# Fewer products of zeros ahead of the first FFN block: 33 in place of 60

## The chip, the cores and the metric

The kernel runs on one core of a Trainium2 chip. Its time is the device time of one execution in microseconds (us); lower is better. The median of three runs of the kernel before is 180.96 us (180.59 to 181.47).

## What is computed

Windowed attention with a few global keys, and then a feed-forward network (FFN) that takes the largest of three products:

```python
# q, k, v: 4 batches x 8 heads x 768 x 64; n_global = 8, n_local = 96
keep = is_global | is_local                  # key < 8, or 0 <= query - key < 96
scores = q @ k.T / 8 - slope[head] * dist    # dist: distance, 96 for a global key out of the window
a = softmax(where(keep, scores, -1e9))
x = (a @ v) with the heads side by side      # 3072 x 512
h = maximum(maximum(x @ w1, x @ w2), x @ w3) # 3072 x 768
out = h @ w_out                              # 3072 x 512, float32
```

## The kernel before, in words

The 3072 rows are 24 tiles of 128 queries, six to a batch. A tile needs its own 128 keys and those of the tile before it; the global keys are copied over rows of the tile before that no query of the tile can see. FFN work goes by chunks of 4, 2, 2, 4, 4, 4 and 4 tiles, so that one weight block meets up to 512 rows at once.

No planner runs at build time. The whole order of the work is one string, `SCHEDULE` (lines 24 to 86), and the last loop (lines 518 to 524) issues its units one after the other. Each unit is a letter for a function, its arguments, and behind an @ the slot of the ring of buffers that it takes. Every engine works off its own instructions in this order; between engines, semaphores hold an instruction until its inputs are there and its buffer is free. The loads are all issued from SP's queue, also in this order.

The units that the steps below speak of:

- `l` loads q, k or v (lines 182 to 195), `w` a weight (455 to 460). `c` and `v` cast them to bf16 (197 to 213); `W` casts a slice of a weight (462 to 464), W1.2 the middle block of the third weight.
- `x` transposes q or k on TensorE (PE) through an identity (219 to 233), and `y` copies the result out of PSUM (235 to 244). For the first two pairs of tiles, four rows at a time lie side by side and the tile is called tpq.
- `S` makes scores of four heads (a group g) of one tile T: S1.0 is group 0 of tile 1 (279 to 296). Where its last argument is 1 ("biased"), two products with the identity first put the distance bias into PSUM. `e` takes the exponential on ScalarE (ACT) (298 to 303). `m` multiplies by a mask on VectorE (DVE), and only where the group was not biased (305 to 313).
- `V` copies the global rows of v into a tile's v, on ACT or GpSimd (POOL) (268 to 275). `A` multiplies the weights of a tile by its v and the v of the tile before (326 to 341), `n` divides by the sums on DVE (343 to 350), `t` transposes the result on PE and `u` copies it to xT (359 to 367).
- `F` is one FFN product of a chunk: four matmuls into one PSUM bank (374 to 380). `f` takes it out of PSUM, as a copy or as a maximum (387 to 399). `O`, `o` and `s` are the product with w_out, its copy and its store.
- `D` and `d` are products of zeros: n matmuls of a constant tile of zeros into a PSUM bank that nobody reads, of the ring h or, for `d`, of the ring sp:

```python
def u_D(slot, n, w, name="h"):
    wp = ring(name, slot, [128, 512 if name == "h" else 1024], FP32, "wp")
    for _ in range(n):
        nc.tensor.matmul(wp[:, 0:w], zeros[:, 0:128], zeros[:, 0:w], start=True, stop=True)
```

D5.256@3 so is five matmuls of 256 columns into slot 3 of h. The ring h has four PSUM banks, which transposes, FFN products and zeros share; the ring sp has two double banks, which scores and attention outputs share. A product into a bank that another instruction last wrote or read waits for that instruction.

Of the kernel before, what the change touches and what calls it, by code (L numbers as in the profile page):

```python
# [22 lines left out]

SCHEDULE = """
    l1.12.0@0 l0.12.0@1 R K3 K7 K4 B1.0 K2 K6 K1 K0 K5 B5.1 B3.1 B0.0 c1.12.0.1@0 B2.1 l1.12.1@2 l0.12.1@3
    c0.12.0.1@1 B7.1 l2.0.2@0 v1.0.2 v0.1.2 l2.1.2@1 v0.0.2 l1.2.2@4 D10.512@0 D2.256@1 x12.1.0@1 y0.1.0.0@0
    v1.1.2 y1.1.0.1@1 D5.256@2 x12.0.0@2 l0.2.2@5 y0.0.0.0 S0.0.1@0 c1.12.1.1 e0.0@0 d7.256@1 S1.0.0@1
    w0.0@0 c0.12.1.1 v3.1.2 w0.1@1 x12.1.1@3 D7.256@0 x12.0.1@0 v2.1.2 e1.0@1 y0.1.1.0 w0.2@2 y0.0.1.0
    d6.256@0 S0.1.0@0 G0.0 e0.1@2 v3.0.2 S1.1.0@1 v2.0.2 c1.2.2.2@2 e1.1@3 w1.0@0 y1.1.1.1 y1.0.0.1 y1.0.1.1
    w1.1@1 l2.2.2@2 G1.1 D4.256@1 S2.0.1@0 e2.0@4 m0.1.1 D6.256@1 A0@1 m1.0.1 n0@0 D4.256@1 S2.1.0@0 m1.1.1  # L30
    G2.0 e2.1@5 D2.256@1 S3.1.0@1 t0@1 m2.1.1 e3.1@6 u0.1@0 D5.256@3 A1@0 n1@1 S3.0.1@1 c0.2.2.1 l0.3.2@6
    V1.0 D7.256@3 A2@0 V2.2 x2.1.2@3 e3.0@7 w1.2@2 m3.1.1 x2.0.2@2 y2.1.2.0@2 A3@1 n2@2 W0.1.2 V3.2 t2@0
    n3@3 u2.1 y2.0.2.0 W0.0.2 t1@1 D5.256@3 t3@3 W2.0.2 G3.0 u1.0 l1.3.2@0 u3.1 B4.0 S4.0.0@0 S4.1.0@1
    e4.1@0 G4.0 W1.1.2 v4.1.2 q2@1 m4.1.1 e4.0@2 W0.2.0 F0.0.1@2 F0.1.1@0 F0.1.0@1 F0.0.0@3 f0.1.0.1@0
    l2.3.2@0 m4.0.1 f0.0.0.0@1 S5.1.0@1 v4.0.2 S5.0.0@0 F0.0.2@1 f0.1.1.1 F0.1.2@3 F0.4.0@0 e5.0@1 f0.0.1.1
    f0.0.2.1@0 f0.1.2.1 W1.0.0 e5.1@3 m5.0.1 W2.1.1 l1.4.2@1 F0.5.0@2 f0.5.0.1@2 c0.3.2.2@0 v5.0.0 v5.1.0
    F0.3.0@1 F0.2.0@3 f0.2.0.1@3 f0.3.0.0@4 F0.2.1@2 f0.2.1.1 A4@0 n4@0 W1.2.2 F0.5.1@3 m5.1.1 f0.5.1.1
    f0.4.0.0@1 F0.4.1@1 v7.0.2 t4@0 F0.3.1@2 x3.0.2@3 V4.0 f0.3.1.1 W2.2.0 A5@1 y3.0.2.0@3 u4.1@1 n5@2
# [519 lines left out]
```

## Time and profile before

| | us |
|---|---|
| median of three runs | 180.96 (180.59 to 181.47) |
| the profiled execution, in all | 180.58 |
| its span, from the first to the last instruction | 178.8 |
| TensorE busy | 170.8 (96%) |
| VectorE busy | 131.4 (73%) |
| ScalarE busy | 107.7 (60%) |
| GpSimd busy | 43.1 (24%) |
| zero products (L478): 10 of 512 columns, 60 of 256 | 12.1 busy, first start 1.2, last 23.4 |
| FFN products (L379), 504 | 99.6 busy, first start 24.75 |

Times are counted from the first instruction of the span. Matmuls are pipelined and their ends are modelled, so the distance from start to start tells what one costs. "Idle before" is the time in which an engine had nothing running, with what ended it. The chain of work is followed back from the last instruction, at each step to what released it; in it, "issue" is time in which an engine waited for nothing that the profile shows. PEclk is the clock that TensorE was granted, as a share of the full one.

### The profile page before, as it was taken

The numbers are of one execution on the slowest core, as the hardware profiler recorded it, in microseconds if no ns is written. First come the engines' busy times: TensorE is split into PE (matmuls) and PEld (weight loads), VectorE is DVE, ScalarE is ACT, GpSimd is POOL, SyncE is SP. The second block draws the span as 40 slices with busy tenths as digits, with TensorE's granted clock in tenths as the row PEclk, the third lists the DMA queues.
The fourth block names the chain that finished last, engine by engine and source line by source line (L and its number), as shares of the span: only waits on it lengthen the run. The fifth ranks groups of instructions, "written<-read, shape, count | busy, mean of one in ns | idle before, by whom it ended". The sixth has DMA issues, their size and how long they took to land.

```text
span 178.8 us, 3957 instructions
## 1 busy us (share of the span) xinstructions
PE 170.8 (96%) x1552; PEld 96.8 (54%) x1552; DVE 131.4 (73%) x258; ACT 107.7 (60%) x166; POOL 43.1 (24%) x72
## 2 busy tenths in 40 slices
PE   7699999999999999999999999999999999999692
PEld 2376764466876776844545544644445464444242
DVE  6558958988697979775899668997768984355800
ACT  5968898675899958866589587336154733110022
POOL 3049285427034453000202701130101040000000
PEclk9999999999999999999999999999999999999999
DMA  4999999999984999499999789997990142460006
GB/s 148 351 291 316 366 370 322 344 297 339 293 214 97 197 242 176 96 349 290 194 299 225 144 153 278 248 207 236 229 175 11 33 146 59 176 235 4 0 22 215
DMA packets 66627, 37.49 MB, mean 210 GB/s; under 512 B 24624, under 2 KB 61360, under 8 KB 66608
## 3 DMA queue, kind: packets, MB, share of 16 engines
q1 hardware_dynamic: 66464, 37.17, 83.5%
q8 instruction: 12, 0.20, 0.5%
q10 hardware_dynamic: 144, 0.07, 0.1%
q14 instruction: 7, 0.06, 0.1%
HBM read 25.17 MB, written 6.29 MB: 176 GB/s over the span
## 4 chain that ended last, share of the span: by engine, by line
PE 89%; ACT 3%; issue 2%; DVE 2%; POOL 1%; ACTq 0%
PE h L379 53%; PE po L403 18%; PE sp L295 7%; PE op L337 3%; PE wp L478 3%; PE op L340 3%; ACT wmask L324 2%; PE tp L233 1%; PE xtp L364 1%; PE tpq L227 1%; POOL qb L208 1%; ACT qkT L241 1%; ACT bias L319 0%; POOL va L273 0%; DVE ht L398 0%
## 5 line engine op out<-in xcount | busy, mean ns | idle before, releaser
L379 PE MATMUL h<-xT,w 128*128 128x512 bf16 (+1 forms) x504 | 99.6, 349 | 0.1
L379 PEld LDWEIGHTS <-w 128*128 128x128 bf16 x504 | 47.3, 98 | 42.0 <-issue 1.0
L302 ACT ACTIVATE P<-sp 128x1024 bf16<-128x1024 f32 (+1 forms) x48 | 43.9, 952 | 14.2 <-PE sp L295 13.8
L403 PE MATMUL po<-wo,ht 128*128 128x512 bf16 (+2 forms) x156 | 33.9, 363 | 1.5 <-DVE ht L398 1.5
L311 DVE TENSOR_TENSOR P<-P,wmask 128x1024 bf16<-128x1024 bf16 x38 | 28.7, 766 | 7.3 <-ACT P L302 7.2
L395 DVE TENSOR_TENSOR h<-h,h 128x512 bf16<-128x512 bf16 (+1 forms) x42 | 25.1, 606 | 10.1 <-PE h L379 7.6
L398 DVE TENSOR_TENSOR ht<-h,h 128x512 bf16<-128x512 bf16 (+1 forms) x42 | 26.4, 646 | 4.2 <-PE h L379 3.2
L393 ACT CAST h<-h 128x512 bf16<-128x512 f32 (+1 forms) x24 | 12.6, 538 | 20.9 <-PE h L379 20.7
L403 PEld LDWEIGHTS <-ht 128*128 128x128 bf16 x156 | 13.9, 98 | 15.8 <-DVE ht L398 2.0
L213 POOL CAST va<-rawv 64x512 bf16<-64x512 f32 x20 | 13.2, 664 | 28.6 <-DMA rawv<-in_v_dram 27.9
L349 DVE TENSOR_TENSOR xb<-op,rz 128x512 bf16<-128x512 f32 x24 | 16.6, 692 | 0.8
L393 DVE CAST h<-h 128x512 bf16<-128x512 f32 (+1 forms) x18 | 10.7, 597 | 8.3 <-PE h L379 8.0
L273 POOL COPY va<-vaf 4x260 int32<-4x260 int32 x20 | 8.8, 439 | 30.9 <-PE op L340 27.0
L295 PE MATMUL sp<-qkT 64*128 64x128 bf16 x352 | 14.7, 218 | 0.7 <-ACT qkT L241 0.6
L295 PEld LDWEIGHTS <-qkT 64*128 64x128 bf16 x352 | 10.0, 94 | 9.0 <-issue 6.3
L418 ACT COPY ost<-po 128x512 f32<-128x512 f32 x15 | 8.8, 587 | 8.5 <-PE po L403 8.3
L337 PEld LDWEIGHTS <-P 128*128 128x128 bf16 x192 | 12.5, 97 | 2.1 <-issue 0.2
L478 PE MATMUL wp<-zeros 128*128 128x256 bf16 (+1 forms) x70 | 12.1, 312 | 1.2 <-DVE cap L496 1.2
L337 PE MATMUL op<-va,P 128*128 128x65 bf16 x160 | 12.5, 193 | 0.0
L340 PEld LDWEIGHTS <-P 128*128 128x128 bf16 x160 | 10.5, 97 | 1.6
L340 PE MATMUL op<-va,P 128*128 128x65 bf16 x128 | 9.9, 193 | 0.1
L408 ACT COPY ost<-po 128x512 f32<-128x512 f32 (+2 forms) x5 | 2.3, 480 | 12.3 <-PE po L403 12.2
(69 smaller groups left out, 130.0 us busy)
## 6 DMA issues: line engine op xcount, KB each, us to landing
rawv<-in_v_dram SPq DMA_DIRECT2D x12, 512.0 KB, 8.0
out_dram<-ost SPq DMA_DIRECT2D x23, 256.0 KB, 2.5
rawk<-in_k_dram SPq DMA_DIRECT2D x10, 512.0 KB, 7.3
rawq<-in_q_dram SPq DMA_DIRECT2D x10, 512.0 KB, 7.4
wst<-in_moe_w_dram SPq DMA_DIRECT2D x3, 1024.0 KB, 10.3
wst<-in_moe_w_dram SPq DMA_DIRECT2D x3, 512.0 KB, 8.2
wost<-in_moe_w_out_dram SPq DMA_DIRECT2D x3, 512.0 KB, 6.6
rawqk<-in_k_dram SPq DMA_DIRECT2D x2, 512.0 KB, 5.0
```

The lines of the kernel that those rows point to most:

```text
L295: nc.tensor.matmul(sp[:, hh, j2, ds], qT(T - ds, 1)[hsl, jp], qT(T, 0)[hsl, jp], start=not how, stop=True, skip_group_check=True)
L302: nc.scalar.activation(P[:, :, 0:n], sps[T, g].rearrange("p a b d n -> p (a b) d n")[:, :, 0:n], AF.Exp, bias=0.0, scale=scale)
L311: mul(P, P, wmask[:, g, :, 0:2])
L337: nc.tensor.matmul(o, P[:, i, 0], heads(va(T))[:, h], start=True, stop=(t == 0), skip_group_check=True)
L340: nc.tensor.matmul(o, P[:, i, 1], heads(va(T - 1))[:, h], start=False, stop=True, skip_group_check=True)
L349: nc.vector.tensor_tensor(out=x.rearrange("p (g h) d -> p g h d", g=2), in0=o4[:, :, :, 0:64], in1=rz[:, :, :, None].to_broadcast([128, 2, ...
L379: nc.tensor.matmul(ps, w123[f // 2][:, j, dm, (f % 2) * 128:(f % 2) * 128 + 128], xT[c][:, dm], start=(dm == 0), stop=(dm == 3))
L393: copies[how](h01, ps)
L395: nc.vector.tensor_max(h01s[c, f], h01s[c, f], ps)
L398: nc.vector.tensor_max(dst, h01s[c, f].rearrange("p (t e i) -> p t e i", e=2, i=64), ps.rearrange("p (t e i) -> p t e i", e=2, i=64))
L403: nc.tensor.matmul(po, ht[c][:, f, tt * 128:(tt + 1) * 128], wo[:, f, cols], start=(f == 0), stop=(f == NF - 1))
L478: nc.tensor.matmul(wp[:, 0:w], zeros[:, 0:128], zeros[:, 0:w], start=True, stop=True)
```

## The change

Only counts in the schedule are changed. Eleven of the twelve units of 256-column zeros that stood ahead of the first FFN product are left, ten of them with a smaller count; d7 on slot 1 of sp, which stood between the exponential of tile 0's biased group and the scores of tile 1, is gone. The first unit, ten products of 512 columns, stays. In the order in which PE meets them:

| stands ahead of | before | after |
|---|---|---|
| first transposes of k (x12.1.0) | D2 | D1 |
| first transposes of q (x12.0.0) | D5 | D3 |
| scores S1.0, behind the biased S0.0 | d7 | none |
| transposes x12.0.1 | D7 | D5 |
| scores S0.1 | d6 | d4 |
| scores S2.0 | D4 | D3 |
| attention product A0 | D6 | D2 |
| scores S2.1 | D4 | D3 |
| scores S3.1 | D2 | D2 |
| attention product A1 | D5 | D4 |
| attention product A2 | D7 | D2 |
| transposes t3 | D5 | D4 |
| in all | 60 | 33 |

The diff, cut to the lines with a changed unit (the others only move a line break):

```diff
-    c0.12.0.1@1 B7.1 l2.0.2@0 v1.0.2 v0.1.2 l2.1.2@1 v0.0.2 l1.2.2@4 D10.512@0 D2.256@1 x12.1.0@1 y0.1.0.0@0
-    v1.1.2 y1.1.0.1@1 D5.256@2 x12.0.0@2 l0.2.2@5 y0.0.0.0 S0.0.1@0 c1.12.1.1 e0.0@0 d7.256@1 S1.0.0@1
-    w0.0@0 c0.12.1.1 v3.1.2 w0.1@1 x12.1.1@3 D7.256@0 x12.0.1@0 v2.1.2 e1.0@1 y0.1.1.0 w0.2@2 y0.0.1.0
-    d6.256@0 S0.1.0@0 G0.0 e0.1@2 v3.0.2 S1.1.0@1 v2.0.2 c1.2.2.2@2 e1.1@3 w1.0@0 y1.1.1.1 y1.0.0.1 y1.0.1.1
-    w1.1@1 l2.2.2@2 G1.1 D4.256@1 S2.0.1@0 e2.0@4 m0.1.1 D6.256@1 A0@1 m1.0.1 n0@0 D4.256@1 S2.1.0@0 m1.1.1
-    G2.0 e2.1@5 D2.256@1 S3.1.0@1 t0@1 m2.1.1 e3.1@6 u0.1@0 D5.256@3 A1@0 n1@1 S3.0.1@1 c0.2.2.1 l0.3.2@6
-    V1.0 D7.256@3 A2@0 V2.2 x2.1.2@3 e3.0@7 w1.2@2 m3.1.1 x2.0.2@2 y2.1.2.0@2 A3@1 n2@2 W0.1.2 V3.2 t2@0
-    n3@3 u2.1 y2.0.2.0 W0.0.2 t1@1 D5.256@3 t3@3 W2.0.2 G3.0 u1.0 l1.3.2@0 u3.1 B4.0 S4.0.0@0 S4.1.0@1
+    c0.12.0.1@1 B7.1 l2.0.2@0 v1.0.2 v0.1.2 l2.1.2@1 v0.0.2 l1.2.2@4 D10.512@0 D1.256@1 x12.1.0@1 y0.1.0.0@0
+    v1.1.2 y1.1.0.1@1 D3.256@2 x12.0.0@2 l0.2.2@5 y0.0.0.0 S0.0.1@0 c1.12.1.1 e0.0@0 S1.0.0@1 w0.0@0
+    c0.12.1.1 v3.1.2 w0.1@1 x12.1.1@3 D5.256@0 x12.0.1@0 v2.1.2 e1.0@1 y0.1.1.0 w0.2@2 y0.0.1.0 d4.256@0
+    S0.1.0@0 G0.0 e0.1@2 v3.0.2 S1.1.0@1 v2.0.2 c1.2.2.2@2 e1.1@3 w1.0@0 y1.1.1.1 y1.0.0.1 y1.0.1.1 w1.1@1
+    l2.2.2@2 G1.1 D3.256@1 S2.0.1@0 e2.0@4 m0.1.1 D2.256@1 A0@1 m1.0.1 n0@0 D3.256@1 S2.1.0@0 m1.1.1 G2.0
+    e2.1@5 D2.256@1 S3.1.0@1 t0@1 m2.1.1 e3.1@6 u0.1@0 D4.256@3 A1@0 n1@1 S3.0.1@1 c0.2.2.1 l0.3.2@6 V1.0
+    D2.256@3 A2@0 V2.2 x2.1.2@3 e3.0@7 w1.2@2 m3.1.1 x2.0.2@2 y2.1.2.0@2 A3@1 n2@2 W0.1.2 V3.2 t2@0 n3@3
+    u2.1 y2.0.2.0 W0.0.2 t1@1 D4.256@3 t3@3 W2.0.2 G3.0 u1.0 l1.3.2@0 u3.1 B4.0 S4.0.0@0 S4.1.0@1 e4.1@0
```

On ACT, DVE, POOL and SP the instructions and their order are the same as before.

More of the change, by code (lines that the diff above doesn't have):

```diff
@@ L25 @@
     l1.12.0@0 l0.12.0@1 R K3 K7 K4 B1.0 K2 K6 K1 K0 K5 B5.1 B3.1 B0.0 c1.12.0.1@0 B2.1 l1.12.1@2 l0.12.1@3
-    c0.12.0.1@1 B7.1 l2.0.2@0 v1.0.2 v0.1.2 l2.1.2@1 v0.0.2 l1.2.2@4 D10.512@0 D2.256@1 x12.1.0@1 y0.1.0.0@0
-    v1.1.2 y1.1.0.1@1 D5.256@2 x12.0.0@2 l0.2.2@5 y0.0.0.0 S0.0.1@0 c1.12.1.1 e0.0@0 d7.256@1 S1.0.0@1
-    w0.0@0 c0.12.1.1 v3.1.2 w0.1@1 x12.1.1@3 D7.256@0 x12.0.1@0 v2.1.2 e1.0@1 y0.1.1.0 w0.2@2 y0.0.1.0
-    d6.256@0 S0.1.0@0 G0.0 e0.1@2 v3.0.2 S1.1.0@1 v2.0.2 c1.2.2.2@2 e1.1@3 w1.0@0 y1.1.1.1 y1.0.0.1 y1.0.1.1
-    w1.1@1 l2.2.2@2 G1.1 D4.256@1 S2.0.1@0 e2.0@4 m0.1.1 D6.256@1 A0@1 m1.0.1 n0@0 D4.256@1 S2.1.0@0 m1.1.1
-    G2.0 e2.1@5 D2.256@1 S3.1.0@1 t0@1 m2.1.1 e3.1@6 u0.1@0 D5.256@3 A1@0 n1@1 S3.0.1@1 c0.2.2.1 l0.3.2@6
-    V1.0 D7.256@3 A2@0 V2.2 x2.1.2@3 e3.0@7 w1.2@2 m3.1.1 x2.0.2@2 y2.1.2.0@2 A3@1 n2@2 W0.1.2 V3.2 t2@0
-    n3@3 u2.1 y2.0.2.0 W0.0.2 t1@1 D5.256@3 t3@3 W2.0.2 G3.0 u1.0 l1.3.2@0 u3.1 B4.0 S4.0.0@0 S4.1.0@1
-    e4.1@0 G4.0 W1.1.2 v4.1.2 q2@1 m4.1.1 e4.0@2 W0.2.0 F0.0.1@2 F0.1.1@0 F0.1.0@1 F0.0.0@3 f0.1.0.1@0
-    l2.3.2@0 m4.0.1 f0.0.0.0@1 S5.1.0@1 v4.0.2 S5.0.0@0 F0.0.2@1 f0.1.1.1 F0.1.2@3 F0.4.0@0 e5.0@1 f0.0.1.1
+    c0.12.0.1@1 B7.1 l2.0.2@0 v1.0.2 v0.1.2 l2.1.2@1 v0.0.2 l1.2.2@4 D10.512@0 D1.256@1 x12.1.0@1 y0.1.0.0@0
[6 more added lines that the diff above has]
+    u2.1 y2.0.2.0 W0.0.2 t1@1 D4.256@3 t3@3 W2.0.2 G3.0 u1.0 l1.3.2@0 u3.1 B4.0 S4.0.0@0 S4.1.0@1 e4.1@0
+    G4.0 W1.1.2 v4.1.2 q2@1 m4.1.1 e4.0@2 W0.2.0 F0.0.1@2 F0.1.1@0 F0.1.0@1 F0.0.0@3 f0.1.0.1@0 l2.3.2@0
+    m4.0.1 f0.0.0.0@1 S5.1.0@1 v4.0.2 S5.0.0@0 F0.0.2@1 f0.1.1.1 F0.1.2@3 F0.4.0@0 e5.0@1 f0.0.1.1
     f0.0.2.1@0 f0.1.2.1 W1.0.0 e5.1@3 m5.0.1 W2.1.1 l1.4.2@1 F0.5.0@2 f0.5.0.1@2 c0.3.2.2@0 v5.0.0 v5.1.0
```

## The prediction

> **What bounds the kernel now.** I read the windows view first, cut at the first FFN product (24.75 us) and at the last one before the tail (168.56). Its columns are the stretch, its length, then busy time (instructions) of PE, PEld, DVE, ACT and POOL, the granted clock, DMA share and GB/s.
>
> ```profile
> 0.00:24.75 24.75, 21.69 (x269) 14.64 (x269) 18.13 (x48) 19.40 (x34) 11.36 (x24) 1.00 1.00 304
> 24.75:168.56 143.81, 143.78 (x1248) 79.11 (x1248) 111.56 (x207) 86.03 (x128) 31.73 (x49) 1.00 0.85 201
> 168.56:178.80 10.24, 5.38 (x36) 3.02 (x36) 1.71 (x3) 2.29 (x5) 0.00 (x0) 0.96 0.30 103
> ```
>
> In the middle stretch TensorE is idle 0.03 of 143.81 us: from the first FFN product on it is the bound, so whatever moves the start at 24.75 moves the end. The zero products all lie ahead of it. The chain of work that ended last (start, length, what) tells which of them count:
>
> ```profile
> 9.03 0.88 PE wp L478 x7
> 9.91 0.04 issue
> 9.96 0.40 PE sp L295 x8
> 10.36 0.55 PE tpq L227 x8
> 10.91 0.78 PE wp L478 x7
> 11.69 0.04 issue
> 11.73 0.61 PE tpq L227 x8
> 12.34 0.67 PE wp L478 x6
> 13.01 0.04 issue
> 13.05 0.51 PE sp L295 x12
> ```
>
> From 9.03 on the zero products stand in the chain itself: PE, not its inputs, is late. Last, the timelines of DVE and POOL around the masking products (start, length, instruction):
>
> ```profile
> 16.77 1.03 POOL L208 CAST qb<-rawk 128x1024 bf16<-128x1024 f32 x1
> ...
> 16.85 1.50 DVE L311 TENSOR_TENSOR P<-P,wmask 128x1024 bf16<-128x1024 bf16 x1
> ```
>
> The same DVE product takes 0.68 at 20.64, where POOL has nothing running. Here it ends 0.55 after POOL's cast (17.80 to 18.35); at 25.79 it ends 0.54 after the cast that ends at 26.11. So a masking product that meets a running POOL instruction waits for its end and then takes 0.54.
>
> **The change, part by part.** 27 products of 128x256 go. They start 0.109 apart (seven from 8.96: 0.94 to the end of the last, which itself lasts 0.27, the median of the 70), so 2.95 us of PE. Every other instruction keeps its place on its engine.
>
> *Three go ahead of 7.5 us* (D2 to D1, D5 to D3). There the transposes wait for DVE's casts (idle 0.46 before 5.54, 0.34 before 7.05): this cover hides 0.33 us wholly, and the idle time grows. Gain 0; if the casts came earlier, at most 0.33.
>
> *Twenty-four go between 9.0 and 23.4* (53 become 29), 2.62 us. I followed the engines' orders with the durations of the timelines, noting at each step what is late next; before, then after:
> - S1.0 9.96, 8.87 (d7 is gone; nothing else uses sp bank 1). Its exponential now waits for e0.0, which ends at 9.67: 10.39, 9.57 (ACT starts about 0.10 before the end of the one before).
> - x12.1.1 waits for DVE's cast (8.85 + 0.69): 10.29, 9.58. Then D5; x12.0.1 writes the same bank and starts 0.33 after the start of its last zero product: 11.73, 10.80.
> - ACT's copy y0.0.1 12.37, 11.44; S0.1 13.05, 12.11, now behind that copy and not behind d4. Gain 0.94.
> - e0.1 13.37, 12.43; S2.0's bias waits for it: 14.02, 13.08; S2.0 14.54, 13.60; e2.0 14.98, 14.04. S2.1 waits for e2.0: 16.33, 15.12. S3.1 16.98, 15.76; A1 18.10, 16.77; V1 on ACT 18.89, 17.66, ending 18.93.
> - DVE: m0.1 14.00, 13.06; m1.0 ends 15.68, 14.45; n0 waits for A0: 16.00, 14.61, a gain of 1.39. m1.1 ends 16.13. m2.1 waits for e2.1 (16.64) and meets POOL's cast of v2, which I put at 16.65 to 17.26, so it ends at 17.80 instead of 18.95. Gain 1.15: POOL's casts begin with a landing at 11.23 that does not move, so DVE runs into more of them. n1 ends 20.13, 18.97.
> - A2 waits for n1 and V1: 20.44, 19.02 (D7 became D2). Gain 1.42.
> - V2 on POOL starts behind A2 (19.77 instead of 21.19), but DVE's m3.1 (20.64, 19.49 to 20.17) holds it up: its second copy ends 22.04, 20.89. Back to 1.15.
> - A3 22.09, 20.94; n3 22.75, 21.60; t3 23.75, 22.60; u3 24.18, 23.03; the first FFN product 24.75, **23.60**.
>
> So of 2.62 us taken off PE, 1.15 is gain and the rest becomes waiting. Bounds: with no such collision of DVE and POOL the gain is A2's 1.42. If m2.1 also waits for the next cast (c1.2.2, then 17.30 to 18.33), m2.1 ends at 18.87 and 0.1 is left. I take 1.15, since the rule of the 0.54 fits each row that I tried.
>
> *Behind 24.75* nothing is changed, but PE asks 1.15 earlier for loads that do not move. POOL's casts that end a wait for DMA, and their users on PE: the second weight's middle block (W1.1) done 28.95, used 34.17; v4 31.05 and 35.03; q of group 3 32.38 and 38.33; the third weight's (W1.2) 35.04 and 39.34. The least slack is 3.98, far over 1.15. One stall may go: the product at 34.17 waited 0.14 for DVE (33.45 + 0.68), whose queue was late since the product at 28.14 met POOL's cast W1.1 (27.91 to 28.95); begun at 26.99 it would miss it. So 1.15 to 1.29: I take **1.2**.
>
> The profiled execution took 180.58 (178.8 span and 1.78 around it): 179.4. It is the lowest of the times known; the median of the runs is 0.38 above. The runs to come should lie between 179.4 and 179.8: **179.6**.
>
> **The clock.** The zero products also keep PE busy, and PEclk tells what an idle PE costs (stretch, length, PE busy, clock, DMA):
>
> ```profile
> 167.80:171.20 3.40, 1.86 (x10) 1.00 0.01 2
> 171.20:174.60 3.40, 3.40 (x20) 1.00 0.15 55
> 174.60:178.00 3.40, 0.85 (x14) 1.00 0.74 254
> 178.00:178.80 0.80, 0.00 (x0) 0.51 0.00 0
> ```
>
> After 3.4 us with 0.85 busy the clock is about half; after 1.86 busy it is not. In 5.0 to 8.4, PE is busy 2.25 of 3.40 (before); without D3's two and D1's one, near 2.0. In 6.5 to 9.9 it is 2.36 before; d7 (0.94) goes and S1.0 and x12.1.1 (0.35 more) move in, so near 1.8. Both are close to the row that stayed at 1.00, and far from 0.85: I expect no loss.
>
> The Trainium skill speaks against the change here. "TensorE: Matmul & The Clock Gate", Part 1, has the clock fall to half after an idle window of about 3.4 us, and the last two rows agree with that. Its Part 4 says that transposes do not count as busy in the same way; by that rule 5.0 to 8.4 would hold little that counts, and the time would be that of the clock rival below. No run here shows transposes alone.
>
> **The rivals.**
> 1. *The collisions of DVE and POOL cost more* (the 0.1 bound up to 0.8). For: POOL's cast at 16.65 and m2.1 at 16.67 are a near tie. Against: ties cost one cast at most in every row. 180.96 less 0.5: 180.5.
> 2. *The gain is given back behind 24.75*, at a load or at a DVE queue that moved against POOL's casts. For: DMA share 0.85. Against: slacks of 3.98. 180.8.
> 3. *The clock halves for one window* (8.4 to 11.8). Cold products of 128x512 start 0.43 apart (weight loads at 2.02 and 2.44), warm ones 0.22, so what streams takes double. On the path lie two sets of transposes and D5 (0.45 + 0.55 + 0.45): about 1.1 late. 180.7.
> 4. *The clock halves for two windows* (8.4 to 15.2): **slower**. The path then holds 2.4 us of streaming (the above, two bias products 0.43, S0.1, S2.0 and S2.1 some 0.5), all doubled: 179.6 + 2.4 = 182.0. It decides if the busy time of some window falls to where the gate closes, between 0.85 and 1.86 of 3.40, and the next window is not dense enough to open it. Against: PE is at least 70% busy from 9 us on.
>
> **How the numbers follow.** Forecast 0.46; rival 1 0.22; rival 2 0.07; rival 3 0.10; rival 4 0.15. A measurement of this kernel can tell about 0.5%, 0.9 us, from no change: under 180.06 is faster, over 181.86 slower. The forecast's spread (179.1 to 180.1) is nearly all faster, rivals 1 to 3 are the same, rival 4 is slower: 0.45, 0.39, 0.16. The range goes from a gain of 1.5 off the fastest run (179.0) to 181.3, past rivals 1 to 3, and leaves out rival 4 and a little at the low end.
>
> **What would show it.** Right: 43 zero products of both widths; S1.0 at about 8.9; A2 at 19.0 and A3's second product at 20.9; the first FFN product at 23.6; PE idle next to nothing from there to a last product 1.2 earlier; PEclk at 1.00 throughout. Wrong: transposes 0.11 apart and PEclk under 1.00 in some slice (the clock); a masking product over 1.5 us long between 15 and 18 (rival 1); the first product at 23.6 but the end not earlier (rival 2).

## The result, and the profile after

| | before | after |
|---|---|---|
| median of six runs on one chip, us | 180.88 (180.59 to 181.47) | 179.62 (179.29 to 179.99) |
| ratio of the two | | 0.9931, 95% interval 0.991 to 0.9952 |
| the profiled execution, us | 180.58 | 179.93 |
| its span | 178.8 | 178.2 |
| first FFN product starts | 24.75 | 23.37 |
| last FFN product starts | 168.15 | 167.52 |

The change makes the kernel 0.7% faster; 179.6 was forecast. A ratio, here and below, leaves out a run that lies more than 1.5% above the fastest of its kernel (one run in each of three kernels below). The profiled pair differs by 0.65 only, the medians by 1.26: the execution profiled before is as short as the shortest of its runs, the one profiled after is near the top of its own, and below it is shown what it lost.

The windows view of the changed kernel, cut at its first FFN product and behind its last one; the tail is left out. The columns are those shown with the prediction.

```profile
0.00:23.37 23.37, 19.71 (x242) 12.36 (x242) 17.46 (x48) 19.23 (x34) 12.48 (x24) 1.00 0.99 298
23.37:167.93 144.56, 143.76 (x1248) 79.19 (x1248) 110.55 (x207) 86.10 (x128) 33.14 (x49) 1.00 0.87 204
```

The head is 1.38 shorter. But the middle stretch, in which TensorE idled 0.03 us before, now has 0.80 of idle (144.56 less 143.76). So part of the gain was given back behind the head.

The chain of work that ended last, from the same stretch as the one shown of before:

```profile
9.59 0.62 PE tpq L227 x8
10.21 0.56 PE wp L478 x5
...
10.81 0.62 PE tpq L227 x8
...
11.46 0.59 ACT qkT L241
...
12.10 0.51 PE sp L295 x12
```

One unit of zeros (L478) is left in this stretch, the D5 ahead of x12.0.1, where three held the chain before. (Behind it, up to the first FFN product, the chain holds one more unit, the D3 at 12.61, where it held five before.) S0.1 now starts behind ACT's copy (L241), not behind zeros: PE waits for its inputs.

The timelines of DVE and POOL at the masking product m2.1 (start, length, instruction):

```profile
16.66 0.69 DVE L311 TENSOR_TENSOR P<-P,wmask 128x1024 bf16<-128x1024 bf16 x1 [0.46 <-ACT P L302]
...
15.70 2.12 POOL L213 CAST va<-rawv 64x512 bf16<-64x512 f32 x2
```

The second of the two v casts starts at 16.73, 0.07 behind m2.1. So m2.1 went first and took 0.69, and this time POOL's cast was the one that waited: 1.09 where it took 0.61 before.

Where the 0.80 went, by the chain of work further on (start, length, what):

```profile
81.81 7.91 DMA qkT<-qb
...
89.76 0.62 PE sp L295 x16
```

The scores of tile 14 (S14) waited for X14: the units X transpose a tile's q and k by a DMA that SP issues (line 249, qkT<-qb; from tile 4 on). It goes out at 81.81 and lands 7.91 later; the waits view puts 0.8 on it. What comes ahead of X14 is SP's queue. Its timeline before, and then after:

```profile
76.24 2.32 SPq L195 DMA_DIRECT2D rawv<-in_v_dram  x1
78.61 3.36 SPq L195 DMA_DIRECT2D rawq<-in_q_dram  x2
82.13 3.76 SPq L249 DMA_TRANSPOSE qkT<-qb  x1
```

```profile
78.28 3.36 SPq L195 DMA_DIRECT2D rawq<-in_q_dram  x2
81.81 3.75 SPq L249 DMA_TRANSPOSE qkT<-qb  x1
```

Each line begins 0.05 to 0.17 behind the end of the one before: SP issues without a pause, each DMA holds it for some time (up to 3.8 us), and X14 goes out when its turn comes. PE would have asked for X14's data 1.5 earlier than before; SP came to it 0.32 earlier, and it landed 0.16 earlier (89.72 for 89.88), since it took 7.91 for 7.75. Before, S14's first weights were loaded at 90.36: a slack of 0.4 to 0.5. The gain of 1.52 (1.38 and the stall of 0.14 at 34.17, which is gone) less the 0.16 less this slack leaves about 0.9 of waiting; 0.8 was measured.

The gain in the head alone does not make this wait. SP comes to X14 at a different time in each execution: at 80.97 to 81.81 in the profiles of the changed kernel and of the two kernels below that keep a part of its short zeros, at 82.13 and 82.18 in two profiles of the kernel before, at 83.21 and 83.63 in its two halves, whose heads gained next to nothing and which waited 0.3 and 0.6 at S14 all the same.

### The profile page after: what moved, and what is told of

It is laid out like the page before. It is cut to its first block, busy times and chain, and to the rows that moved or that the text cites. A ratio compares the mean times of both kernels' runs of the same rounds, so it can differ in the third digit from the quotient of the medians.

```text
span 178.2 us, 3903 instructions
## 1 busy us (share of the span) xinstructions
PE 168.9 (95%) x1525; PEld 94.6 (53%) x1525; DVE 129.7 (73%) x258; ACT 107.6 (60%) x166; POOL 45.6 (26%) x72
## 4 chain that ended last, share of the span: by engine, by line
PE 77%; DMA 8%; ACT 5%; DVE 4%; issue 2%; POOL 1%; SPq 1%; ACTq 0%
PE h L379 45%; PE po L403 18%; PE sp L295 6%; DMA qkT<-qb 4%; DMA rawk<-in_k_dram 3%; PE op L337 3%; PE op L340 2%; ACT wmask L324 2%; ACT P L302 2%; PE tp L233 1%; PE tpq L227 1%; POOL va L273 1%; ACT qkT L241 1%; PE xtp L364 1%; SPq L195 1%
## 5 line engine op out<-in xcount | busy, mean ns | idle before, releaser
L311 DVE TENSOR_TENSOR P<-P,wmask 128x1024 bf16<-128x1024 bf16 x38 | 26.6, 708 | 7.9 <-ACT P L302 7.8
L213 POOL CAST va<-rawv 64x512 bf16<-64x512 f32 x20 | 15.1, 757 | 29.4 <-DMA rawv<-in_v_dram 19.2
L478 PE MATMUL wp<-zeros 128*128 128x256 bf16 (+1 forms) x43 | 9.8, 360 | 1.2 <-DVE cap L496 1.2
```

The source lines that it names most:

```text
L213: copies[how](heads(va(T))[64 * e:64 * e + 64, :, 0:D], src)
L311: mul(P, P, wmask[:, g, :, 0:2])
```

## The experiments

The theory to be tested: the gain is what the followed steps say, zeros on PE up to S0.1 and then the masking products' place against POOL's casts. Its rivals: the gain is that of d7 or of the other zeros alone; the clock decides; the DMAs behind the head decide. Beside each group stands the time of before on the same chip. Only the schedule was edited, and all that any of these kernels leaves out is products of zeros that nobody reads.

**The change in two halves** (before: 180.97, 29 runs). First d7 alone goes:

```diff
- y1.1.0.1@1 D5.256@2 ... e0.0@0 d7.256@1 S1.0.0@1
+ y1.1.0.1@1 D5.256@2 ... e0.0@0 S1.0.0@1
```

> The kernel before with one part of the change alone: the seven products of d7 are gone, all other zeros keep their old counts. Theory (the zeros stand on the path, and each part counts by itself): S1.0 at 8.9, the transposes x12.0.1 at 11.02 in place of 11.73, and the 0.71 then stays up to the first FFN product, at 24.05 in place of 24.75; the time 180.2. Rival (the path is held by DVE and ACT, and the PE time won ahead of 12 us turns into waiting): the first FFN product stays within 0.2 of 24.75 and the time at 180.9. Clock rival: PEclk falls under 1.00 between 8 and 15 us and the time is 181 or more.

180.77 (180.41 to 181.61, 12 runs), ratio 0.9995 [0.998, 1.001]. PE gained up to S0.1 (12.35 for 13.05), but the first FFN product stood at 24.63: 0.11 of 0.70 was left. The theory had all of it left; the rival, that the time won turns into waiting, came true. DVE and POOL of this kernel:

```profile
17.18 1.66 DVE L311 TENSOR_TENSOR P<-P,wmask 128x1024 bf16<-128x1024 bf16 x1 [0.34 <-ACT P L302]
...
17.27 1.03 POOL L208 CAST qb<-rawk 128x1024 bf16<-128x1024 f32 x1
```

m2.1 starts 0.09 ahead of the k cast, while a v cast still runs (to 17.32), and lets both go first: it ends at 18.84, 0.54 behind the k cast's end. Then the other half, everything but d7:

```diff
- ... e0.0@0 S1.0.0@1
+ ... e0.0@0 d7.256@1 S1.0.0@1
```

> The changed kernel with d7 back, so the other part of the change alone. Theory: S1.0 is back at 9.96, but D5 and d4 are shorter than D7 and d6, so S0.1 starts at 12.8 in place of 13.05, and D2 ahead of A0 and of A2 gives more: the first FFN product at 24.0, the time 180.2; the two parts add up to about the whole. Rival (d7 alone carries the change): the first FFN product at 24.7 and 180.8.

180.98 (180.57 to 181.74, 12 runs), ratio 1.0005 [0.9991, 1.0018]; first FFN product 24.71 where 24.0 was expected. S0.1 did start at 12.80, as expected: up to there the two halves add up (0.70 and 0.25, and 0.95 for the whole change). The same two timelines:

```profile
17.36 1.56 DVE L311 TENSOR_TENSOR P<-P,wmask 128x1024 bf16<-128x1024 bf16 x1 [0.44 <-ACT P L302]
...
17.34 1.03 POOL L208 CAST qb<-rawk 128x1024 bf16<-128x1024 f32 x1
```

m2.1 comes 0.02 behind the k cast and ends at 18.92. In before and in both halves the first FFN product starts 5.79 behind the end of m2.1 (18.955 and 24.749, 18.841 and 24.634, 18.922 and 24.715). So d7 alone is worth 0.11, the rest alone 0.04, and both together 1.38; the first two are less than the 0.33 by which two profiles of the kernel before differ here (last run of the third group). Behind S0.1 the halves do not add up, because what decides is whether m2.1 starts ahead of POOL's last two casts (16.66) or into them (17.18, 17.36); before, m1.1 met the k cast (16.85) and m2.1 stood behind it.

**Taking POOL's k cast out of the way** (before: 181.08, 23 runs). Beside these ran the changed kernel once more:

> The changed kernel once more, beside the three below. The product m2.1 on DVE started 0.07 before POOL's cast in its profile, and the clock rival has not shown in six runs. Theory: 179.6, all runs within 179.2 to 180.2. Clock rival: some of the runs fall to half clock for one window and end at 180.7 or later. Tie rival (a landing that comes 0.1 earlier lets POOL's cast go first): two groups of runs, 0.5 to 1.0 apart.

179.33 (179.0 to 179.37, 4 runs), ratio 0.9893 [0.9873, 0.9913]: on this chip the change gains 1.1%, where the first measurement had 0.7%. First FFN product 23.38; m2.1 again went ahead of the v cast (16.67 and 16.72), and S14 waited 0.2. The cast that m2.1 meets goes from POOL to DVE, behind m2.1, in the kernel with d7 back:

```diff
- v2.0.2 c1.2.2.2@2 e1.1@3
+ v2.0.2 e1.1@3
- S3.0.1@1 c0.2.2.1
+ S3.0.1@1 c1.2.2.1@2 c0.2.2.1
```

> The changed kernel with d7 back, and with the cast of k of group 2 on DVE behind n1 in place of POOL, so that POOL has no cast at 17.35 to 18.38 for m2.1 to wait for. Theory (that cast, not PE, cost this kernel its gain): m2.1 ends at 17.9 in place of 18.92, the first FFN product comes at 24.0 to 24.1 in place of 24.71, 180.4 in place of 181.0. Rival (PE's zeros hold the path, the collision lies beside it): 24.7 and 181.0.

180.78 (180.33 to 183.05, 12 runs), ratio 0.9985 [0.9966, 1.0003]. First FFN product 24.44 for 24.71: less came than the 0.6 to 0.7 expected. DVE and POOL:

```profile
16.46 1.60 DVE L311 TENSOR_TENSOR P<-P,wmask 128x1024 bf16<-128x1024 bf16 x2
...
20.35 0.69 DVE L311 TENSOR_TENSOR P<-P,wmask 128x1024 bf16<-128x1024 bf16 x1
...
20.35 1.39 POOL L273 COPY va<-vaf 4x260 int32<-4x260 int32 x2 [3.51 <-issue]
```

The two masking products end at 18.06, so m2.1 ends 0.86 earlier, where the theory had 1.0. But the added cast makes m3.1 late enough to fall on POOL's copy V2, which took 0.95 for 0.40 and kept the next attention product. One collision was traded for another. In the changed kernel the same edit should cost little:

> The same move of that cast in the changed kernel. Theory: m2.1 got ahead of POOL's casts there, so nothing is to be won; DVE has 0.6 more to do between n1 and m3.1, and the first FFN product comes at 23.4 to 23.7: 179.6 to 179.9. Rival (the cast costs every kernel the same): the first FFN product at 22.7, 179.0.

179.70 (179.18 to 181.45, 12 runs), ratio 0.9937 [0.9908, 0.9965]; first FFN product 23.55, inside what was expected. Its profiled run, one of the three slowest with 181.32, waited for such transposing DMAs: 1.2 at 62.53 and 0.8 at 91.17. The other two, 181.27 and 181.45, have no profile.

**What the zeros are for** (the first two: before 180.97; the other two: before 181.00, 11 runs). All 33 short ones go from the changed kernel:

```diff
- D10.512@0 D1.256@1 x12.1.0@1
+ D10.512@0 x12.1.0@1
...
```

> The changed kernel without its last 33 products of 256 columns; the ten of 512 at the start stay. Theory (the clock stays open, what is left is on the path in part): the transposes x12.0.1 start at 10.2, S0.1 at 11.6, V1 at 17.1, the first FFN product at 23.0 (23.4 in the changed kernel): 179.3, or 179.6 if the wait for the transposing load near 90 us takes it back. Clock rival: a window of 3.4 us ahead of 12 us holds too little, PEclk falls to half in it, and the time is 180.4 to 181.7.

181.04 (179.45 to 182.41, 12 runs), ratio 0.9987 [0.9958, 1.0016]: five runs from 179.45 to 180.13, seven from 180.86 to 182.41. Windows of the profiled one (181.70), cut where the granted clock was set:

```profile
8.08:11.50 3.42, 1.82 (x29) 1.24 (x28) 2.30 (x4) 3.04 (x7) 0.20 (x1) 1.00 1.18 302
11.50:14.91 3.41, 2.92 (x30) 1.67 (x31) 3.16 (x7) 2.30 (x5) 3.26 (x5) 0.50 1.20 291
...
21.74:25.15 3.41, 3.23 (x39) 2.97 (x38) 1.72 (x4) 2.42 (x4) 2.60 (x6) 0.50 1.06 387
25.15:28.56 3.41, 3.30 (x31) 1.78 (x31) 1.25 (x3) 3.24 (x6) 2.35 (x3) 1.00 1.15 312
```

After a window with 1.82 busy the clock fell to half and stayed there for four windows, 13.65 us, with PE busy 2.61 to 3.23 of each 3.41. The first FFN product came at 26.07, 2.70 late. The Trainium skill, "TensorE: Matmul & The Clock Gate", Part 1, describes such a free-running window of about 3.4 us, and has the clock open behind one busy window. The length agrees; here the clock opened behind the busiest of the four, 3.23, and not behind 2.92, 2.92 and 2.61.

Every run also has its mean granted clock on record. One window of 3.41 at half clock lowers that mean by about 0.01 (half of 3.41, over 178). Of these twelve runs three have 0.99, four 0.98, two 0.97 and two 0.96, which is about one, two, three and four such windows, and only one has 0.999. So the clock closed in at least eleven of the twelve, in four of the five short ones too; those with one window took 179.45 to 180.13, those with two 179.96 to 182.07, those with three or four 181.60 to 182.41. In every run of the kernels that keep at least the changed kernel's zeros ahead of 12 us the mean is 0.996 or more. Then the ten long zeros go as well:

```diff
- D10.512@0 x12.1.0@1
+ x12.1.0@1
```

> The changed kernel without any product of zeros, the ten of 512 columns too. Theory: PE starts at half clock, its transposes stand 0.11 apart; from 9 us on PE is dense enough that the clock opens within one or two windows of 3.4 us, and 1 to 2 us are lost against the kernel without the short ones: 180.3 to 181.3. Rival (the clock opens only in the FFN products): every product ahead of 24 us takes double, the first FFN product is 3 to 5 us late, and the time 183 to 185. Rival (the zeros never mattered for the clock): as without the short ones, 179.3.

182.07 (181.83 to 182.22, 5 runs), ratio 1.006 [1.0044, 1.0076]: slower than the 181.3 that the theory allowed. Two stretches of PE's timeline, attention products of 65 columns:

```profile
17.64 0.24 PE L337 MATMUL op<-va,P 128*128 128x65 bf16 x1
17.69 0.25 PE L340 MATMUL op<-vaf,P 128*128 128x65 bf16 x1
...
20.33 0.19 PE L337 MATMUL op<-va,P 128*128 128x65 bf16 x1 [0.25 <-DVE xb L349]
20.36 0.19 PE L340 MATMUL op<-va,P 128*128 128x65 bf16 x1
```

They start 0.05 apart, and from 20.33 on 0.03 apart: without the long zeros the clock opened only at 19.92, again behind a window (16.51 to 19.92) that was busier, 3.37, than the three ahead of it (2.62 to 2.70). The first FFN product came at 24.80, and waits of 0.3 at 85.77, 0.3 at 111.63 and 0.6 at 112.55 followed. Next, which of the 33 matter. With the 20 behind 12 us gone, only D10, D1, D3, D5 and d4 are kept:

```diff
- D3.256@1 S2.0.1@0 e2.0@4 m0.1.1 D2.256@1 A0@1
+ S2.0.1@0 e2.0@4 m0.1.1 A0@1
...
```

> The changed kernel with its zeros ahead of 12 us (D1, D3, D5, d4) and without the twenty behind them. Theory (behind 12 us the waits for ACT, DVE and POOL set the pace, the zeros lie beside them, and PE is dense enough for the clock): the first FFN product stays at 23.3 to 23.4, the clock is open from about 5 us on, 179.3 to 179.7. Clock rival: some window behind 12 us holds as little as the 1.82 of 3.42 us at which the clock closed without any short zeros, it halves, and the time is 181 to 182. Rival (the twenty are still on the path): the first FFN product at 23.0 or less, 179.2.

179.78 (179.06 to 180.07, 6 runs), ratio 0.9938 [0.9924, 0.9952]. The window of its head:

```profile
0.00:23.37 23.37, 16.92 (x221) 10.51 (x222) 17.54 (x48) 19.16 (x34) 12.56 (x24) 1.00 1.00 298
```

PE is busy 2.79 less in the head, and the first FFN product starts at the same 23.37: these 20 stood beside other work, and cost and gave nothing. This profiled execution took 179.06, and its last FFN product started at 166.63, 1.52 earlier than before: the whole gain of the head, with no wait at S14. SP had come to X14 at 80.97, 1.16 earlier than before. The other half goes:

```diff
- x12.1.1@3 D5.256@0 x12.0.1@0 ... d4.256@0 S0.1.0@0
+ x12.1.1@3 x12.0.1@0 ... S0.1.0@0
...
```

> The changed kernel without its thirteen zeros ahead of 12 us, and with the twenty behind them. Clock theory (the thin stretch is 5 to 11.5 us, and these thirteen hold it over the point where the clock closes): in part of the runs the clock halves between 8 and 12 us, as without any short zeros; runs fall into two groups, about 179.3 and 181 to 182, and the median is 180 to 181.5. Path theory (x12.0.1 at 10.2 and S0.1 at 11.6 without them, and the clock stays): the first FFN product at 23.0, 179.2 in all runs.

179.48 (179.03 to 182.06, 6 runs), ratio 0.9926 [0.9901, 0.9951]; first FFN product 23.22 in the profiled one (179.42), where 23.0 was expected. Four runs lie from 179.03 to 179.53, two at 180.66 and 182.06. The window behind the opening of its clock:

```profile
5.72:9.13 3.41, 1.88 (x30) 1.25 (x28) 1.85 (x4) 3.03 (x8) 0.00 (x0) 1.00 1.11 342
```

1.88 was just enough this time. The two long runs have no profile, but their mean granted clocks are on record: 0.981 (180.66) and 0.991 (182.06), where the other four have 0.996 to 1.0. So the clock closed in both, for about two windows and for one; where in the run, and why the one cost more than the two, is not shown. The two groups of runs are those of the clock theory, but the median stayed with the short ones. Last, the kernel before once more:

> The kernel before once more, for a second profile. Theory: as in the first one the first FFN product comes at 24.7 to 24.8, and the product that meets POOL's cast of k takes 1.5 us. If the spread of its times comes from waits for the transposing loads behind 60 us, this profile has such waits where its time is over 180.9.

180.76, with a first FFN product at 25.08 and a last one at 168.33. Its head was 0.33 worse than that of the profiled before, its end only 0.18, and behind the head PE had no wait. The head was late from the clock on: the long zeros stand 0.43 apart up to 5.43 (in the first profile up to 3.72, and 0.21 from 4.05 on), so the clock opened only at 7.03 in place of 3.93, and the first transposes, 0.11 apart, started at 6.21 in place of 5.54. The product that met POOL's k cast took 1.29, not the 1.5 expected, and ended 0.55 behind that cast.

**What gives the gain back.** X14 goes out ahead of the loads of q for the groups 8 and 9, behind which it stood (before: 181.08):

```diff
- l0.8.2@4 F3.2.2@2 ... l0.9.2@3 X14@3
+ X14@3 l0.8.2@4 F3.2.2@2 ... l0.9.2@3
```

> The changed kernel with the transposing load of group 7 (X14) issued ahead of the loads of q of groups 8 and 9, behind which it stood. Theory (part of the gain is given back at the scores of tile 14, which waited 0.84 for this load in the profile): the wait is gone and the time is 179.0 to 179.2. Rival (DMA as a whole is late there): the wait turns up at the next scores or FFN chunk, 179.6. Rival (only the profiled execution had the wait): 179.6 with no wait in the profile.

179.68 (179.05 to 180.06, 6 runs), ratio 0.9908 [0.9885, 0.9932]; 179.0 to 179.2 was expected, and the changed kernel took 179.33 beside it. The wait at S14 fell to 0.1, but the chain shows another of 0.4 at tile 10, in a stretch that the edit does not touch:

```profile
55.76 5.72 DMA qkT<-qb
...
61.52 0.51 PE sp L295 x11
```

So X10 and X14 were both brought forward, and the cast ahead of X10 with it (before, on another chip: 180.78, 14 runs):

```diff
- c1.5.2.2@2 v9.1.2 ... O0.1@0 c0.5.2.1 F1.0.2@2 ... l0.6.2@6 ... v11.0.1 X10@1 V8.2
+ c1.5.2.2@2 c0.5.2.1 v9.1.2 ... O0.1@0 F1.0.2@2 ... X10@1 l0.6.2@6 ... v11.0.1 V8.2
```

> The changed kernel with both transposing loads brought forward that scores were seen to wait for: X14 ahead of l0.8.2 as in after_x14_early, and X10 ahead of l0.6.2, with the cast that it needs moved ahead of a bias cast on DVE. Theory (what the change gains by the first FFN product is given back only at these two loads): X10 is issued near 54.7 in place of 55.7, the scores of tiles 10 and 14 start without a wait over 0.1, the first FFN product stays at 23.4, and the time falls to 178.8 to 179.1, below the 179.3 to 179.7 of the changed kernel. Rival one (the loads of these stages are late as a whole, and a load moved forward delays the one that is moved back): a wait of 0.3 to 0.8 turns up at another load behind 42 us, and the time stays at 179.4 to 179.7. Rival two (the DVE cast in its new place delays the chain of the FFN group near 52 us): a stall of PE there, and 179.8 or more.

179.68 (179.05 to 180.83, 9 runs), ratio 0.9942 [0.9917, 0.9967]. Its chain:

```profile
75.52 5.15 DMA rawk<-in_k_dram
...
82.97 0.06 ACT qb L208
...
84.03 0.63 ACT vaf L213
...
84.70 0.19 PE op L340
```

No wait at tiles 10 and 14, but 0.4 at the attention product at 84.70 and 0.5 at the scores at 104.83, and no gain in time: the outcome that rival one had. The chain ends the k load at 80.67, but the last part of it landed at 82.9 (7.4 behind its issue, by the view of this tile); ACT cast it at 82.97, and the v cast behind it ended at 84.66. SP came to the k load at 75.52, 0.98 later than in the changed kernel (74.54). That the moved DMAs made it late is not shown: in six kernels that moved none SP came to it at 75.26 to 75.73, and d7_back and d7_back_k_on_dve waited 0.2 at the same product. What the two edits show is that waits for these DMAs turn up at other places and that the time stays. The way to test this further, fewer or shorter DMAs on SP between 60 and 82 us, was not tried.

## Why the prediction came out as it did

| start of | predicted | measured |
|---|---|---|
| S1.0 | 8.87 | 8.87 |
| x12.1.1, x12.0.1 | 9.58, 10.80 | 9.59, 10.81 |
| S0.1 | 12.11 | 12.10 |
| S2.0, S2.1 | 13.60, 15.12 | 13.60, 15.11 |
| S3.1 | 15.76 | 15.77 |
| A1 | 16.77 | 16.77 |
| end of m2.1 | 17.80 | 17.35 |
| A2 | 19.02 | 18.68 |
| end of V2's second copy | 20.89 | 20.67 |
| t3 | 22.60 | 22.36 |
| first FFN product | 23.60 | 23.37 |

- **The zeros ahead of 13 us: right.** d7 and the D5 and d4 that took the places of D7 and d6 gave the 0.94 (0.95 measured), step by step.
- **m2.1 and POOL: the rule was right, the tie fell the other way.** That a masking product ends 0.54 behind the POOL cast it meets held in both halves. The Trainium skill, "SBUF — State Buffer", section "Who interferes with whom", says that VectorE with two SBUF inputs and GpSimd share a port pair that whoever comes first holds for the whole instruction; 16.66 against 16.73 agrees, with the cast stretched to 1.09; with d7 alone gone, m2.1 came first by 0.09 as well, but while the cast ahead was still running, and there the k cast went next. The near tie fell this way in all six profiles in which m2.1 came at 16.65 to 16.67, by 0.05 to 0.13. Of the 0.45 that m2.1 gained on the forecast A2 kept 0.34 and the steps behind it 0.22 to 0.24: the first copy of V2 still had to wait for m3.1 (0.70 for 0.40).
- **The gain of the head: mis-sized.** 1.15 was taken, 1.38 measured, inside the bounds of 0.1 and 1.42. The lower bound was real: m2.1 had to come 0.5 later for 0.1 to be left, and both halves show it.
- **The stall at 34.17: right.** It is gone, 0.14.
- **"The least slack is 3.98": wrong.** Only the loads that POOL casts were looked at, not the transposing DMAs. X14's slack was 0.4 to 0.5, and SP's queue sets when it goes out. The profiled execution gave back 0.8 of 1.52, which is rival 2, by a DMA that was not looked at; in the profile of early_kept nothing was given back, and the halves waited there without a gain to give. So the wait belongs to the spread of the executions as much as to the change; what moves SP's queue by 1 us from one execution to the next stays open.
- **179.6 and 179.62 agree by more than the working does.** From the profiled execution 179.4 was worked out, and 179.93 came; the 0.23 that the head gave more and the 0.8 that X14 took are both missing in it, so that the two agree is luck in part. Over the runs, the medians gained 1.26 where 1.2 was summed.
- **The clock: right that it stays, wrong in the prices.** The lowest window in the head of the changed kernel was well above the 1.8 that was worked out for 6.5 to 9.9:

```profile
6.34:9.75 3.41, 2.39 (x35) 1.61 (x33) 2.43 (x5) 3.03 (x8) 0.00 (x0) 1.00 1.13 333
```

Rivals 3 and 4 counted one or two cold windows; without the short zeros there were one to four by the mean clock, and in the profiled run four, 2.70 us at the first FFN product. The prediction held 1.8 busy to be safe; 1.82 was not.

## What to carry to other kernels

A chain through two engines that share something has steps in it: work out on which side of a tie the change lands, and do not add up the halves. When the start of a long stretch moves forward, list what each queue must deliver in it, and by when; the DMAs of a queue that issues without a pause need not come along (X14 came 0.32, 0.91 and 1.16 earlier in three profiles whose heads were 1.4 shorter). Padding is worth its place only in the windows where the busy time would otherwise fall too low: here the 20 later zeros could go for nothing, and the 13 early ones, taken away with the 20, cost about 1.3 us (181.04 against 179.78, ratios 0.9987 [0.9958, 1.0016] and 0.9938 [0.9924, 0.9952]); taken away alone they left the median where it was, with two long runs of six, in both of which the clock had closed. No kernel here is shown to be faster than the changed one.

## What the runs showed of the hardware

- The clock closed after a window with 1.82 of 3.42 us busy, and stayed open after 1.86 of 3.40 (before) and 1.88 of 3.41 (late_kept). Once closed it stayed so for 13.65 us with PE busy over three quarters of the time: windows of 2.61 to 2.92 did not open it again, one of 3.23 did (no_short_zeros). The busy time alone does not decide: in the kernel before 2.74 of 3.41, long zeros without a gap, had opened it (products 0.43 apart up to 3.72, 0.21 from 4.05 on).
- Between 50 and 92 us, over all profiles, SP is held by a transposing DMA of q and k for 1.2 to 4.5 us, by a plain one for 0.4 to 3.7, and the transposing ones land 3.6 to 7.9 us after their issue.
- The clock first opened at 3.93 to 7.03 us in the profiles with the long zeros: the same kernel (before, before_again) had it at 3.93 and at 7.03, and its first FFN product at 24.75 and at 25.08.
- In the kernel without zeros the granted-clock column reads 1.00 from the start, while the spacing of the products (0.05 and then 0.03) shows half the clock up to 19.92: the column knows nothing ahead of its first record.
